# An attention and mixer kernel on one core: the first batch's v by casting transfers of GpSimd, later loads, shared PSUM tiles and whole-block squares

## The chip, the core and the metric

The kernel runs on one core of a Trainium2 chip. The core has five engines with a queue of instructions each: TensorE (PE, matmuls, with its weight loads shown as PEld), VectorE (DVE), ScalarE (ACT), GpSimd (Pool) and SyncE (SP), which here only issues transfers. Sixteen DMA engines move the data. SBUF is the memory on the core with 128 partitions; PSUM takes the matmuls' sums. The metric is device time in microseconds (us) of one execution.

## The reference

The batch is 8, the sequence S = 3136, the model width D = 256, the width of the queries and keys 64. All inputs and the result are float32; the kernel works in bfloat16 between them.

```python
scale = 1.0 / S
scores = scale * np.matmul(z, z.transpose(0, 2, 1))   # per batch: S x S
attn = np.maximum(scores, 0.0) ** 2
x = u * np.matmul(attn, v)                            # x: S x 256

h = (xT @ U @ V)T                                     # U: S x 32, V: 32 x S
u2 = x + h
result = u2 + np.maximum(u2 @ w_ch1, 0.0) @ w_ch2     # w_ch1: 256 x 1024
```

The keys and the queries are the same z, so the scores are symmetric: a block of keys against queries is the transpose of the mirrored block.

## The kernel before, in words

The 3136 rows of a batch are 24 tiles of P = 128 rows and a tail of 64. Queries go in groups of GW = 512 columns: NQ = 6 full groups and a seventh of 64 (NG = 7 groups to a batch). One pass of the main loop is a *slot* t, a batch and group (b, g); there are 56. In a slot PE computes attention times v for its group, scores for groups to come, and, a batch later, the mixer's part for group t − 7 and t − 8 (x + h, called u2, then w_ch1 and w_ch2).

**Blocks of scores.** A block holds four key tiles by 512 queries, 128x4x512 bf16, and stands in one of 20 SBUF buffers `blk`. It is made in two halves. For each half `score_pairs` runs two matmuls side by side, each on 64 of PE's rows (`pair`, the matmul at L184), into a PSUM tile `ps` of two banks (there are four such tiles). `rectify` then chooses ACT (L399) or DVE (L395) for relu and scale, PSUM to SBUF, and `score_finish` books the half's square on DVE for when the relu is done (`square`, L364, 128x1024). A half can be used by PE once it is squared. In the first slot `rectify` instead takes its ways from a list: "half" (ACT and DVE take one bank each of the same PSUM tile, relu at L376 and L377, square at L380 and L381) for the first two pairs, then "both", then "dve" (`one_pass`, L406: relu and square on DVE).

**The order.** The kernel is written with its own model of time. `clock` counts what PE has been given, `free_at` what the other engines have, `book` adds a piece of work to an engine, and `hold(time, f)` keeps a step back until the clock reaches that time; a step is put in its engine's queue when `run_held` comes to it. The order in which steps are issued is the order in each engine's queue. A queue is worked off in that order, so a transfer at SP that has to wait holds up those behind it. Blocks that are used from their mirrored side are turned by transposing DMAs (`issue_turn`, L421 and L429), and the tile z of later batches too.

**Mixer inputs.** x (L749, DVE, in bf16 as `x_bf`) plus h gives u2; its transpose `u2T` comes from a transposing DMA on SP (`x_turn`, L785), and PE multiplies it with w_ch1. `u2T` of the first group is needed first when slot 7 ends.

**Loads.** SP issues all transfers from device memory. `load_part` loads z and v of the next batch, `load_u` one group's u, `first_loads` the constants: U in slot 2, V in 3 and 4, w_ch1 in 5, w_ch2 in 6 (`load_w`). Up to slot 7 the loads are held to the slot's clock plus 5, and each next one 22 later; u to plus 60. Loads give float32; casts to bf16 are held in the next slot (`casts_next`).

**The first batch.** z comes in three pieces and v in six of four tiles, each staged as float32 in blocks: z (L1274, L226), v (L1274, L256) and the tails of 64 rows (L220) alternate on SP. z is cast on DVE and ACT (first piece), on Pool (second; L242) and on DVE (third). v's six pieces are cast by Pool (`cast_v`, L1261), the first straight away and the others as `spare` steps between other work. PE turns the cast z (`z_turn`, L331) and ACT copies the result into `zzT` (L340). Before that PE runs 21 empty matmuls (L1300). Then three score jobs are issued one by one (L1314 to L1316), and the main loop starts.

A GpSimd `nop` (L174) links two matmuls on different row halves of one PSUM bank; it is put in Pool's queue in the order of issue.

The following listing gives the functions that the change touches.

## Time and profile before

| | us |
|---|---|
| median of 3 runs | 982.09 (981.95 to 982.22) |
| profiled execution, device time | 986.39 |
| its span on the core | 984.6 |
| TensorE busy, share of the span | 973.7 (99%) |
| VectorE busy | 628.2 (64%) |
| ScalarE busy | 482.4 (49%) |
| GpSimd busy | 15.2 (2%) |

Mean granted TensorE clock: 0.998. The profile lists, for groups of instructions by line and operation, the output and input buffer, the sizes, the count, the busy time, and what ended the idle time before them. The chain that ended last follows the work back from the end through whatever released each step. The timeline lists instructions in order with start, duration, engine, line, operation, count, and in brackets how long the engine sat idle before and which piece of work ended it. An engine named with a q is its sequencer: SPq is the issue of transfers from SP's queue. Durations of transfers are given from issue to landing. Times of a timeline count from the start of the span.

### The profile page before, as it was taken

How to read it: one execution, taken by the hardware profiler on the slowest of the kernel's cores; microseconds unless marked ns; L12 is line 12 of the kernel's file. 1: busy time of each engine (PE TensorE's matmuls, PEld its weight loads, DVE VectorE, ACT ScalarE, POOL GpSimd, SP SyncE). 2: the span in 40 equal slices, each digit the busy share in tenths (PEclk: the TensorE clock that was granted, in tenths of full speed). 3: DMA queues.
4: the chain of work that ended last, by engine and by line, in shares of the span. 5: the costliest groups of instructions: out<-in, count | busy, mean ns of one | idle time of the engine just before them, and what ended most of it. 6: DMA issues, size and time to landing. Idle time of an engine off the chain costs nothing.

```text
span 984.6 us, 35373 instructions
## 1 busy us (share of the span) xinstructions
PE 973.7 (99%) x16163; PEld 773.4 (79%) x16163; DVE 628.2 (64%) x811; ACT 482.4 (49%) x565; POOL 15.2 (2%) x25
## 2 busy tenths in 40 slices
PE   8999899999999999999999999999999999999998
PEld 5788677877778778787777877788777887778766
DVE  6878755668556685566755667556775567653363
ACT  7877642456324473355633555334654346431353
POOL 4200000000000000000000000000000000000000
PEclk9999999999999999999999999999999999999999
DMA  8899999979997799987999879997799978965153
GB/s 269 193 225 192 228 196 188 223 153 197 195 204 167 160 192 192 205 170 170 185 208 207 154 178 179 223 189 153 173 207 206 194 144 163 186 135 95 55 114 99
DMA packets 372405, 176.37 MB, mean 179 GB/s; under 512 B 347296, under 2 KB 350624, under 8 KB 372256
## 3 DMA queue, kind: packets, MB, share of 16 engines
q1 hardware_dynamic: 372256, 174.12, 85.6%
q8 instruction: 126, 2.06, 0.9%
q14 instruction: 23, 0.19, 0.1%
HBM read 62.56 MB, written 25.69 MB: 90 GB/s over the span
## 4 chain that ended last, share of the span: by engine, by line
PE 96%; DVE 1%; ACT 1%; DMA 1%; issue 0%; DVEq 0%
PE ps L184 93%; PE ps L714 1%; DMA u2T<-x_bf 1%; PE ps L797 1%; ACT blk L399 0%; PE ps L1096 0%; DVE blk L364 0%; PE ps L1300 0%; PE ps L331 0%; DVE blk L377 0%; DVE blk L381 0%; DVE x_bf L749 0%; DVE blk L406 0%; DVE out_sb L870 0%; DVE blk L395 0%
## 5 line engine op out<-in xcount | busy, mean ns | idle before, releaser
L184 PEld LDWEIGHTS <-blk 64*128 64x128 bf16 x12288 | 609.7, 94 | 159.9 <-POOLq L174 9.6
L184 PE MATMUL ps<-v_bf,blk 64*128 64x256 bf16 x9216 | 613.0, 269 | 2.3 <-DVE blk L364 1.1
L399 ACT ACTIVATE blk<-ps 128x1024 bf16<-128x1024 f32 (+1 forms) x335 | 315.3, 970 | 346.6 <-PE ps L184 343.2
L364 DVE TENSOR_TENSOR blk<-blk 128x1024 bf16<-128x1024 bf16 x350 | 221.1, 656 | 49.1 <-ACT blk L399 48.4
L184 PE MATMUL ps<-u2T,w_bf 64*128 64x512 bf16 (+1 forms) x1792 | 227.9, 350 | 2.8 <-DMA u2T<-x_bf 2.8
L184 PE MATMUL ps<-w_bf,blk 64*128 64x256 bf16 x3072 | 192.0, 269 | 0.0
L959 DVE TENSOR_SCALAR blk<-ps 128x1024 bf16<-128x1024 f32 x105 | 128.5, 1224 | 97.6 <-PE ps L184 96.6
L962 ACT ACTIVATE blk<-ps 128x1024 bf16<-128x1024 f32 x87 | 88.3, 1022 | 119.0 <-PE ps L184 118.8
L184 PE MATMUL ps<-zzT 64*128 64x512 bf16 (+2 forms) x902 | 129.8, 327 | 0.6 <-ACT zzT L340 0.6
L184 PEld LDWEIGHTS <-w_bf 64*128 64x128 bf16 x1792 | 84.3, 94 | 30.2 <-POOLq L174 5.0
L749 DVE TENSOR_TENSOR x_bf<-ps,u_sb 128x1024 bf16<-128x1024 f32 x48 | 58.7, 1222 | 71.4 <-PE ps L184 71.4
L870 DVE TENSOR_TENSOR out_sb<-ps,x_bf 128x1024 f32<-128x1024 f32 x42 | 51.4, 1224 | 58.1 <-PE ps L184 58.1
L1082 DVE TENSOR_TENSOR out_sb<-ps,out_sb 128x1024 f32<-128x1024 f32 x42 | 51.4, 1224 | 18.6 <-PE ps L184 18.3
L184 PEld LDWEIGHTS <-zzT 64*128 64x128 bf16 x902 | 41.2, 94 | 6.9 <-ACT zzT L340 1.5
L184 PE MATMUL ps<-t_sb,V_bf 64*128 64x256 bf16 x200 | 20.6, 269 | 0.0
L395 DVE TENSOR_SCALAR blk<-ps 128x1024 bf16<-128x1024 f32 (+1 forms) x14 | 16.6, 1185 | 5.9 <-PE ps L184 5.1
L206 DVE CAST v_bf<-stage 128x1024 bf16<-128x1024 f32 (+1 forms) x30 | 18.5, 617 | 0.0
L184 PE MATMUL ps<-v_bf,last_sb 64*128 64x256 bf16 x192 | 18.5, 269 | 0.0
L204 ACT CAST v_bf<-stage 128x1024 bf16<-128x1024 f32 (+1 forms) x18 | 18.1, 1005 | 0.0
L206 DVE CAST x_bf<-out_sb 128x1024 bf16<-128x1024 f32 x22 | 15.2, 689 | 0.3
L1082 DVE TENSOR_TENSOR blk<-ps,blk 128x1024 f32<-128x1024 f32 x5 | 6.1, 1225 | 11.9 <-PE ps L184 11.8
L204 ACT CAST x_bf<-out_sb 128x1024 bf16<-128x1024 f32 x13 | 13.5, 1037 | 0.0
(83 smaller groups left out, 239.1 us busy)
## 6 DMA issues: line engine op xcount, KB each, us to landing
u_sb<-in_u_dram SPq DMA_DIRECT2D x48, 512.0 KB, 5.1
stage<-in_v_dram SPq DMA_DIRECT2D x42, 512.0 KB, 6.1
out_dram<-out_sb SPq DMA_DIRECT2D x42, 512.0 KB, 3.1
stage<-in_z_dram SPq DMA_DIRECT2D x7, 512.0 KB, 5.9
blk<-in_v_dram SPq DMA_DIRECT2D x5, 512.0 KB, 6.3
out_dram<-blk SPq DMA_DIRECT2D x5, 512.0 KB, 2.6
blk<-blk SPq DMA_TRANSPOSE x156, 5.1
blk<-in_moe_w_ch_dram SPq DMA_DIRECT2D x4, 512.0 KB, 4.9
```

The source lines that it names most:

```text
L184: ins = nc.tensor.matmul(**args)
L204: nc.scalar.copy(out=out, in_=in_)
L206: nc.vector.tensor_copy(out=out, in_=in_)
L364: nc.vector.tensor_tensor(out=a, in0=a, in1=a, op=ALU.mult)
L395: nc.vector.tensor_scalar(out=dst, in0=src, scalar1=scale, scalar2=0.0, op0=ALU.mult, op1=ALU.max)
L399: nc.scalar.activation(out=dst, in_=src, func=AF.Relu, scale=scale)
L714: nc.tensor.matmul(out=ps[c * hp : c * hp + rows, h, :D], lhsT=smalls[b][h * hp : (h + 1) * hp, place_of(jt), :], rhs=v_bfs[b][h * hp : (h ...
L749: nc.vector.tensor_tensor(out=xs[b, g][:rows, :n, :], in0=four(box["ps"])[:rows, :n, :], in1=u_sbs[b, g][:rows, :n, :], op=ALU.mult,)
L870: nc.vector.tensor_tensor(out=o[:rows, :n, :], in0=four(ps)[:rows, :n, :], in1=x, op=ALU.add)
L959: nc.vector.tensor_single_scalar(out=r, in_=ps[:, :, :gw], scalar=0.0, op=ALU.max)
L962: nc.scalar.activation(out=r, in_=ps[:, :, :gw], func=AF.Relu)
L1082: nc.vector.tensor_tensor(out=o, in0=acc, in1=o, op=ALU.add)
```

## The change

There are five parts.

1. The first batch's v is loaded by Pool's own queue, with the cast from float32 to bf16 done by the transfer: seven transfers (two of 128x512 for the first piece, five of 128x1024), straight into `v_bf`. The staging blocks and Pool's casts of v go. On SP the second and third z pieces, the tails and the first u follow one another.
2. The first two score jobs use `shared_pairs`: the pairs' banks are spread over two PSUM tiles, `a` and `d`, so that ACT takes its bank from `a` and DVE its bank from `d`. The way "half" of `rectify` goes.
3. For blocks of batch 0 of which the first half is finished in slots 1 to 5, the half's square is left out, and after the second half one square covers the whole block (`whole_block`, 128x2048).
4. w_ch2 is loaded in slot 7 instead of 6; a slot's `first_loads` stand ahead of the next batch's steps; in slot 7 the loads are held to the clock plus 78 and each next one 12 later; u is held to plus 5 in slot 6 and to plus 88 in slot 7; the casts in slot 8 to 45, and in slot 7 no longer to 60 but to 15.
5. One of the two casts of the third z piece goes from DVE to Pool.

```diff
-    ways = ["half", "half", "both", "dve"]
+    ways = ["both", "dve"]

+    halves, merged = {}, set()
+
+    def whole_block(n, key, turn):
+        waiting[0] -= 1
+        if n == 2:
+            square(blocks[key][1], 11.7)
+            squared[key] = 2
+        if turn:
+            hold(clock[0] + 7, lambda: ready_turns.append(turn))
+
     def score_finish(made):
...
+            if key and not key[0]:
+                n = halves[key] = halves.get(key, 0) + 1
+                if n == 1 and 0 < slot[0] < NQ:
+                    merged.add(key)
+                if key in merged:
+                    finish = lambda n=n, key=key, turn=turn: whole_block(n, key, turn)
             hold(whole or done, finish)

+    def shared_pairs(jobs):
+
+        (ka, a), (kb, d) = take_ps(), take_ps()
+        for i, (b, g, (J, h)) in enumerate(jobs):
...
+                nc.tensor.matmul(
+                    out=(a if jj == i else d)[:, jj, :],
...
+            dst = blocks[b, g, J][1][:, 2 * h : 2 * h + 2, :]
+            x, y = dst[:, i], dst[:, 1 - i]
+            nc.scalar.activation(out=x, in_=a[:, i], func=AF.Relu, scale=scale)
+            nc.vector.tensor_scalar(out=y, in0=d[:, 1 - i], scalar1=scale, scalar2=0.0, op0=ALU.mult, op1=ALU.max)
+            nc.scalar.activation(out=x, in_=x, func=AF.Square)
+            nc.vector.tensor_tensor(out=y, in0=y, in1=y, op=ALU.mult)
...
-        6: lambda: load_w(1),
+        NG: lambda: load_w(1),
...
     def first_v(i):
-        load_v_piece(0, i, vraw[i][1])
+        for t0 in range(i * GT, (i + 1) * GT, GT // 2 if i == 0 else GT):
+            n = GT // 2 if i == 0 else GT
+            nc.gpsimd.dma_start(out=v_bfs[0][:, t0 : t0 + n, :], in_=rows_of(v[0])[:, t0 : t0 + n, :])
+        v_cast.add((0, i))
...
-    for h in range(2):
-        load_run(vraw[0][1], v[0], D, h * GT // 2, GT // 2)
+    for i in range(NQ):
+        first_v(i)
     first_z(1)
-    first_v(1)
     first_z(2)
-    first_v(2)
-    first_v(3)
...
-    first_v(4)
-    first_v(5)
     load_u(*items[0])
-    cast_v(0, on_pool)
     cast_z(1, 0, on_pool)
     cast_z(1, 1, on_pool)
-    spare += [lambda i=i: cast_v(i, on_pool) for i in range(1, NQ)]
...
-    score_burst(jobs0[:1])
-    score_burst(jobs0[1:2])
+    shared_pairs(jobs0[:2])
     score_burst(jobs0[2:3])
...
-            hold(clock[0] + (90 if g_now == NQ and b_next > 1 else 60 if t == NG else 15 if t >= NQ else 45) + 12 * i, f)
+            hold(clock[0] + (90 if g_now == NQ and b_next > 1 else 45 if t == NG + 1 else 15 if t >= NQ else 45) + 12 * i, f)
...
-        steps += first_loads[t]() if t in first_loads else []
+        steps = (first_loads[t]() if t in first_loads else []) + steps
...
-                hold(clock[0] + 5 + 22 * i, lambda f=f: load(f))
+                hold(clock[0] + (78 + 12 * i if t == NG else 5 + 22 * i), lambda f=f: load(f))
         if t <= NG:
-            hold(clock[0] + 60, lambda t=t: load_u(*items[t + 1]))
+            hold(clock[0] + (5 if t == NQ else 88 if t == NG else 60), lambda t=t: load_u(*items[t + 1]))
...
-                qm.append((20, 0, False, lambda: (cast_z(2, 0, on_dve), cast_z(2, 1, on_dve), book("dve", 0, 8))))
+                qm.append((20, 0, False, lambda: (cast_z(2, 0, on_pool), cast_z(2, 1, on_dve), book("dve", 0, 4))))
```

More of the change, by code (lines that the diff above doesn't have):

```diff
@@ L374, in rectify @@
             way = ways.pop(0) if ways else min(ends, key=lambda w: ends[w])
-            if way == "half":
-                nc.scalar.activation(out=dst[:, 0], in_=src[:, 0], func=AF.Relu, scale=scale)
-                nc.vector.tensor_scalar(
-                    out=dst[:, 1], in0=src[:, 1], scalar1=scale, scalar2=0.0, op0=ALU.mult, op1=ALU.max
-                )
-                nc.scalar.activation(out=dst[:, 0], in_=dst[:, 0], func=AF.Square)
-                nc.vector.tensor_tensor(out=dst[:, 1], in0=dst[:, 1], in1=dst[:, 1], op=ALU.mult)
-                done = max(book("act", ready, 5.2), book("dve", ready, 6.2))
-                return done, max(book("act", ready, 5.2), book("dve", ready, 3.5))
             if way == "dve":
@@ L539, in score_burst, with finish @@
         score_finish(score_pairs(jobs))
+    def shared_pairs(jobs):
+        (ka, a), (kb, d) = take_ps(), take_ps()
+        for i, (b, g, (J, h)) in enumerate(jobs):
+            zzT = zzTs[b]
+            if h == 0:
+                blocks[b, g, J] = take_block()
+            for jj in range(2):
+                key = J * GT + 2 * h + jj
+                nc.tensor.matmul(
+                    out=(a if jj == i else d)[:, jj, :],
+                    lhsT=half(zzT, jj, key * P, P),
+                    rhs=half(zzT, jj, groups[g][0], GW),
+                    start=True,
+                    stop=True,
+                )
+            pe(GW / 256)
+            dst = blocks[b, g, J][1][:, 2 * h : 2 * h + 2, :]
[4 more added lines that the diff above has]
+            nc.vector.tensor_tensor(out=y, in0=y, in1=y, op=ALU.mult)
+            ps_free[ka] = book("act", clock[0] + 3, 5.2)
+            ps_free[kb] = book("dve", clock[0] + 3, 6.2)
+            book("act", 0, 5.2)
+            book("dve", 0, 3.5)
+            def finish(key=(b, g, J)):
+                squared[key] = squared.get(key, 0) + 1
+            hold(max(free_at["act"], free_at["dve"]), finish)
     def place_of(jt):
@@ L1243 @@
     zraw = [(i * 2 * GT, 2 * GT + (i == 2), *stage_block()) for i in range(3)]
-    vraw = [stage_block() for _ in range(NQ)]
     on_act, on_dve, on_pool = nc.scalar.copy, nc.vector.tensor_copy, nc.gpsimd.tensor_copy
     def first_v(i):
-        load_v_piece(0, i, vraw[i][1])
+        for t0 in range(i * GT, (i + 1) * GT, GT // 2 if i == 0 else GT):
+            n = GT // 2 if i == 0 else GT
+            nc.gpsimd.dma_start(out=v_bfs[0][:, t0 : t0 + n, :], in_=rows_of(v[0])[:, t0 : t0 + n, :])
+        v_cast.add((0, i))
     def first_z(i):
@@ L1256, in cast_z @@
         z_copy(0, t0 + lo, hi - lo, raw[:, lo * dqk :], c, copy)
-    def cast_v(i, copy):
-        raw = vraw[i][1].rearrange("p (t d) -> p t d", d=D)
-        for h in range(0, GT, GT // 2):
-            copy(out=v_bfs[0][:, i * GT + h : i * GT + h + GT // 2, :], in_=raw[:, h : h + GT // 2, :])
-        v_cast.add((0, i))
-        give_block(vraw[i][0])
     def cast_tail():
```

## The prediction

> **What bounds the kernel now.** I read the page's busy shares and its chain that ended last, then that chain in order of time, then windows and timelines where it leaves TensorE (PE).

> ```profile
> PE 973.7 (99%) x16163; PEld 773.4 (79%) x16163; DVE 628.2 (64%) x811; ACT 482.4 (49%) x565; POOL 15.2 (2%) x25
> ...
> PE 96%; DVE 1%; ACT 1%; DMA 1%; issue 0%; DVEq 0%
> ```

> PE is busy for 99% of the span and carries 96% of the chain. The change leaves PE's count of matmuls and, but for the first two pairs, nearly all of their order as they are, so it can only act where PE stands still. The matmuls show three such places over 0.8 us before 130 us: after 5.60 (1.10), after 26.34 (1.06) and after 108.43 (2.97), with some lesser ones up to 11.57. All else is cover. The chain (start, us, what) shows the first and the last; the line of dots stands for 91 us:

> ```profile
> 6.13 0.70 DVE blk L377
> 6.85 0.42 DVE blk L381
> 7.28 0.70 DVE blk L377
> 8.00 0.86 DVE blk L381
> 8.86 1.14 DVE blk L406
> 10.03 1.49 DVE blk L364 x2
> 11.57 2.64 PE ps L184 x40
> ...
> 102.97 8.44 DMA u2T<-x_bf
> 111.45 87.65 PE ps L184 x1396
> ```

> From 6.13 to 11.57 VectorE (DVE) runs without a pause and PE starts in earnest when it is done. At 102.97 it is a transfer: the first transpose of x into u2T, 8.44 us.

> **Part 1, the loads round the first x turn.** SyncE's (SP's) timeline, start and duration of each issue:

> ```profile
> 99.10 0.78 SPq L226 DMA_DIRECT2D stage<-in_z_dram  x1
> 99.93 0.42 SPq L1190 DMA_DIRECT2D blk<-in_moe_w_ch_dram  x1
> 100.39 0.50 SPq L226 DMA_DIRECT2D stage<-in_z_dram  x1
> 100.94 1.09 SPq L308 DMA_DIRECT2D u_sb<-in_u_dram  x2
> 102.97 2.25 SPq L785 DMA_TRANSPOSE u2T<-x_bf  x1
> ```

> Five loads (512 KB each, one of 256) go out in the 3 us ahead of the transpose; the last landed at 110.53, the transpose at 111.41. The tile's view gives issue to landing as 2.3 least, 3.6 median, 8.4 most (this one). The windows show the price; columns are us, then busy time of PE, its weight loads, DVE, ScalarE (ACT) and GpSimd (Pool), the granted clock, DMA share, GB/s:

> ```profile
> 108.40:114.50 6.10, 3.34 (x30) 1.74 (x28) 2.33 (x3) 0.42 (x1) 0.00 (x0) 0.72 1.02 176
> 114.50:122.00 7.50, 7.50 (x116) 5.39 (x114) 5.64 (x7) 6.86 (x10) 0.00 (x0) 1.00 0.75 207
> ```

> 30 matmuls took 6.10 us; at the next stretch's rate (116 in 7.50) they take 1.94. So 4.2 us hang on this transfer: 2.8 of stall, and 1.3 because the granted clock fell to 0.72 and pairs took 0.21 us apiece instead of 0.107.

> In the changed program SP's order round it is: one u load (formerly two), last_sb's transpose, one small block transpose, u2T's, and only then w_ch2's halves, u, z's two pieces, u, v. The casts of V and w_ch1 stay ahead. The small transpose's input is ready some 3 us earlier, so u2T's is issued as soon as x_bf is done (102.9) and, at the median of 3.6, lands at 106.5; PE asks at 108.43. **Gain 4.2**, with 1.9 us to spare. What is late next: w_ch2 (asked for at 127.4, issued some 22 us ahead, its loads land in 4.9 in the median), the next batch's z and u, behind it on the same queue; their first users are over 10 us away. Nothing waits.

> **Part 2, whole-block squares.** 19 blocks of batch 0 lose two squares of 128x1024 and get one of 128x2048 after the second half. That saves DVE a fixed cost each (656 ns per 1024 columns in the groups, 0.99 for one of 1600, so I estimate 1.21 for 2048 instead of 1.31), under PE: nothing. What it costs is time ahead: half a block is no longer ready while the other is being scored. I took, for each of the 19, the gap from its second score pair to its first use by PE. All but one have 3.65 to 19 us and need about 3 (relu 1, square 1.2, latencies). The exception is the first:

> ```profile
> 27.57 0.38 PE L184 MATMUL ps<-zzT 64*128 64x512 bf16 x2
> ...
> 28.00 4.77 ACT L399 ACTIVATE blk<-ps 128x1024 bf16<-128x1024 f32 x5 [0.98 <-PE ps L184]
> ...
> 29.05 1.25 DVE L364 TENSOR_TENSOR blk<-blk 128x1024 bf16<-128x1024 bf16 x1 [1.05 <-ACT blk L399]
> ```

> Its second pair runs at 27.57, and PE uses the first half at 28.12. After the change that use waits for ACT's relu (28.00 to 28.98) and the square of 2048 (29.03 to 30.24): PE goes on at 30.25, **a loss of 2.13**. The next such block is used 0.2 to 0.45 late as well, against two stalls there (0.22 and 0.21) that the new one absorbs. **Net cost 2.1**, 1.7 to 2.5. Queued behind the square on DVE is only a relu; behind PE's wait stand score pairs whose ACT and DVE work is thereby early, not late. Low bound: 0, if PE's order or the squares' lets another block go first; nothing I see allows it. Can the clock fall too? The stall of 1.06 left pairs at full rate, that of 2.97 did not; 2.1 lies between, nearer to 1.06: I take nothing and keep +1.4.

> [...]

> **Part 3, the start.** In the chain above, DVE's first relu waits until 6.13 for ACT's read of the same PSUM tile (2.29 idle). Two tiles let it begin when pair 0 is done, at 5.47. Then by the same durations: relu 6.16, square 6.58, second relu (pair 1 waits for the tiles' first readers, about 6.6) 7.31, square 7.75 (0.42; the 0.86 stood beside a Pool cast), one pass to 9.1, two squares to 10.5: PE's 11.57 becomes 10.55, **−1.0**.

> But Pool's queue is now in the way. SP loses seven v issues (3.1 us of 0.43 to 0.5 each), so z's second piece is issued at 1.6 instead of 2.6. Pool gets the seven, casting, and behind them its two casts of that z (1.17 together), which a PE turn, an ACT copy (1.0) and PE's pairs wait for: 2.4 us from cast end 8.59 to pair 10.97. Before, Pool's sum was one v cast and then a wait for z. The page has no casting DMA and no Pool DMA, so the issue cost g is unknown. Bounds: 0.43 (SP's issue) to 1.17 (Pool's pair of casts). With issues from 1.35 the casts end at 2.5+7g: 5.5 at 0.43, 10.7 at 1.17, against 8.59 now. The turn limits the start when 7g exceeds 6.0. At 1.17 the start is 1.2 late after the gain is gone. I take about 0.6 (Pool's single cast is the nearest row), which leaves the DVE chain as the limit.

> [...]

> Next, v itself: PE needs its six pieces at 6.81, 11.57, 13.83, 16.74, 19.77 and 22.45; they landed at 5.2, 9.1, 11.3, 13.0, 14.9 and 16.2, 512 KB per 1.64 us (320 GB/s). Afterwards 3.15 MB on Pool's queue run beside 2.0 to 2.8 MB that SP issues without waiting. At an even half, 160 GB/s, pieces land at about 9.6, 12.9, 16.2, 19 and 20.7: just in time for a start 0.8 earlier. **So I take −0.8.** The price of v's cast on Pool (8.3 us in six pairs) goes; it hid beside PE. DVE gives z's last cast (0.4) to Pool, which is idle then.

> **Part 4, nothing.** Later batches keep their order; the tail from 920 us on is the same.

> **Sum**: −4.2 + 2.1 − 0.8 = −2.9. The profiled execution took 986.39 (span 984.6), 4.3 above the median of 982.09; the sum is 983.5 against it, and by the same difference **979.2** against the median. 0.2%, about 2.0 us, is what a measurement here can tell from no change.

> **Rivals.**
> - Squares cost nothing, since the 27.57 block is covered after all: 982.1 − 4.2 − 1.0 = 976.9. For: other blocks have 3.65 and more. Against: the order of instructions. 0.10.
> - The stall of 2.1 also halves the clock, +1.4: 980.6. For: 0.72 after 2.97. Against: full rate after 1.06. 0.08.
> - u2T's transpose still waits for the queue: the 4.2 stays, 983.4. For: six other SP issues stand near it. Against: none of the five loads is ahead of it. 0.04.
> - Pool's issues or v's transfers run behind by a little: the start changes by +0.2 to +3.9, 980.2 to 983.9, say 981.0. For: the single margins worked out above. 0.17.
> - Slower: Pool's seven issues cost 1.6 us or more apiece. z's second piece is then cast at 13.7 and the start is 4.2 late, which with −4.2 and +2.1 passes 2.0; at 2.0 apiece it is 7.0 late, 987.0. DVE's casts and squares beside Pool are the means: a DVE square took 0.86 beside a Pool cast, 0.42 without, and a Pool pair 2.04 instead of 1.17. The same sign if v comes at under 120 GB/s (the last piece after 26.6). Against: both bounds of g lie below 1.6. 0.17.

> [...]

> **How the numbers follow.** The forecast has 0.44, its own range 978.2 to 980.4 (1.0 less to 1.2 more by the squares' and the start's bounds). Leaving out the slower rival (0.17) above and a little below gives 976.9 to 983.4. Faster by over 0.2% (under 980.1): most of 0.44, the 0.10 and a little of the late start, 0.53. Slower: 0.17. Within: 0.30.

> **What would show it.** Right: u2T's first transpose lands in under 5 us and no PE idle near 108; a PE stall of about 2 us at 27 with the releaser DVE L364, its form 128x2048; DVE's first relu near 5.5; PE's long run from about 10.6. Wrong: v's landing, or Pool's z casts, as what ends PE's waits before 25 us; a granted clock under 1.0 after the stall at 27.

## The result, and the profile after

The change made the kernel slower by 0.4%: 986.49 us in the median of 4 runs (985.99 to 988.01) against 982.02 (981.93 to 982.22), ratio 1.0043 with a 95% interval of 1.0031 to 1.0056. Forecast were 979.2 and a range of 976.9 to 983.4; the time lies outside it, on the side that had 0.17. The profiled execution took 988.01, its span is 986.2.

The page after, busy shares and the chain by engine:

```profile
PE 975.1 (99%) x16163; PEld 775.9 (79%) x16163; DVE 626.6 (64%) x794; ACT 481.7 (49%) x562; POOL 10.3 (1%) x21
...
PE 96%; DVE 1%; ACT 1%; DMA 1%; issue 0%; SPq 0%; DVEq 0%
```

PE is the bound as before. Since its matmuls come in nearly the same order, the start of the n-th matmul after, less that of the n-th before, shows where time goes. Between the two profiled executions that offset is +0.6 at 19 us, +0.4 at 26, +4.0 at 33, −0.4 at 115 (all of u2T's stall gone), +1.3 at 130, +1.6 from 191 on. So the two *profiled* executions differ by 1.6, while the *median* times differ by 4.5. That gap is the main thing to explain, beside the four places. A wait is given here, as in the prediction, as the time from one matmul's start to the next, less the 0.05 us that a matmul takes up (0.11 at half rate). The brackets of the timeline count from the modelled end of the matmul before and give 0.2 to 0.5 less.

**The start.** The chain in order of time, after (start, us, what):

```profile
5.60 0.70 DVE blk L569
6.31 0.04 issue
6.35 0.61 PE ps L558 x2
6.96 3.41 PE ps L184 x28
10.37 0.58 PE ps L331 x8
10.95 0.02 issue
10.97 1.02 ACT zzT L340
```

The stretch from 6.8 to 10.3 (us, then busy time of PE, PEld, DVE, ACT, Pool, the granted clock, DMA share, GB/s), the change first and then, from a run further down, its start alone:

```profile
6.80:10.30 3.50, 3.50 (x30) 2.13 (x26) 2.73 (x5) 2.17 (x4) 0.00 (x0) 1.00 1.15 223
6.80:10.30 3.50, 2.94 (x45) 2.01 (x44) 3.43 (x6) 3.00 (x4) 0.61 (x1) 1.00 1.14 224
```

DVE's first relu starts at 5.60 instead of 6.13, as meant. But pair 1 waits until 6.35 for DVE's read of the shared tile (1.31, or 0.81 idle by the timeline), and then 28 matmuls take 3.41 us: a pair took 0.21 instead of 0.107. Half rate is how PE begins in every kernel here: its first empty matmuls and turns of z take 0.107 apiece, later ones 0.055, and the change from one to the other came between 3.8 and 6.0 us in every profile but that of the change. There it came at 10.37. PE itself is now the chain up to the turn, where before it was DVE.

**The first whole block.** The chain after, from its second half's relu on, PE's timeline at its end, and the windows, the last line that of the kernel before:

```profile
28.38 1.03 ACT blk L390
29.43 1.24 DVE blk L364
30.72 48.22 PE ps L184 x786
```

```profile
30.72 0.31 PE L184 MATMUL ps<-v_bf,blk 64*128 64x256 bf16 x2 [2.05 <-DVE blk L364]
```

```profile
28.40:30.70 2.30, 0.26 (x6) 0.00 (x0) 1.23 (x1) 1.00 (x1) 0.00 (x0) 1.00 0.85 274
30.70:34.30 3.60, 3.58 (x30) 2.17 (x32) 0.46 (x1) 1.94 (x2) 2.03 (x2) 0.53 0.15 58
30.70:34.30 3.60, 3.60 (x56) 2.36 (x54) 3.60 (x6) 3.13 (x5) 1.02 (x2) 1.00 0.09 34
```

PE waits 2.27, near the 2.13 worked out, and then goes on at a granted clock of 0.53: 30 matmuls in 3.60, which before took 56 in the same stretch.

**The first x turn.** SP's timeline after:

```profile
104.01 1.19 SPq L412 DMA_TRANSPOSE blk<-blk  x1
106.97 1.93 SPq L825 DMA_TRANSPOSE u2T<-x_bf  x1
108.95 0.58 SPq L1230 DMA_DIRECT2D blk<-in_moe_w_ch_dram  x1
```

The transpose goes ahead of the loads, and PE's wait for it, 2.97 before, is gone; PE's whole list of waits has one for a u2T, of 0.2, at 190.98. (It is part of the last step in the offset above, from +1.3 to +1.6.)

**A new wait at 127.** SP's, DVE's, ACT's and PE's timelines after:

```profile
114.41 7.33 SPq L420 DMA_TRANSPOSE blk<-blk  x1
121.83 1.21 SPq L412 DMA_TRANSPOSE blk<-blk  x1
123.10 1.97 SPq L220 DMA_DIRECT2D stage<-in_z_dram  x2
125.11 1.24 SPq L220 DMA_DIRECT2D stage<-in_v_dram  x2
```

```profile
121.54 1.22 DVE L999 TENSOR_SCALAR blk<-ps 128x1024 bf16<-128x1024 f32 x1
122.67 0.68 DVE L206 CAST x_bf<-out_sb 128x1024 bf16<-128x1024 f32 x1
126.65 0.75 DVE L206 CAST z_bf<-stage 128x576 bf16<-128x576 f32 x1 [3.29 <-DMA stage<-in_z_dram]
127.32 1.28 DVE L364 TENSOR_TENSOR blk<-blk 128x1024 bf16<-128x1024 bf16 x2
128.52 0.29 DVE L206 CAST v_bf<-stage 128x256 bf16<-128x256 f32 x1
128.72 1.22 DVE L999 TENSOR_SCALAR blk<-ps 128x1024 bf16<-128x1024 f32 x1
```

```profile
126.53 0.67 ACT L204 CAST z_bf<-stage 128x576 bf16<-128x576 f32 x1 [2.31 <-DMA stage<-in_z_dram]
127.10 1.93 ACT L390 ACTIVATE blk<-ps 128x1024 bf16<-128x1024 f32 x2
```

```profile
128.17 1.49 PE L184 MATMUL ps<-w_bf,blk 64*128 64x256 bf16 x24 [1.02 <-ACT blk L390]
130.00 0.61 PE L184 MATMUL ps<-w_bf,blk 64*128 64x256 bf16 x8 [0.34 <-DVE blk L999]
```

The moved z loads drag their 64-row tails with them, which are held another 75 of the kernel's own clock and then queue behind a block's transpose. Two casts that read the tail are already in the queues: DVE stands 3.29 us in front of one, ACT 2.31 in front of the other. The relus behind them that PE needs come late: ACT's (L390) ends a stall of 1.23, the mixer's on DVE (L999) one of 0.55.

### The profile page after: what moved, and what is told of

It is laid out like the page before. It is cut to its first block, busy times and chain, and to the rows that moved or that the text cites. A ratio compares the mean times of both kernels' runs of the same rounds, so it can differ in the third digit from the quotient of the medians.

```text
span 986.2 us, 35349 instructions
## 1 busy us (share of the span) xinstructions
PE 975.1 (99%) x16163; PEld 775.9 (79%) x16163; DVE 626.6 (64%) x794; ACT 481.7 (49%) x562; POOL 10.3 (1%) x21
## 4 chain that ended last, share of the span: by engine, by line
PE 96%; DVE 1%; ACT 1%; DMA 1%; issue 0%; SPq 0%; DVEq 0%
PE ps L184 93%; PE ps L754 1%; PE ps L837 1%; ACT blk L390 0%; PE ps L1136 0%; DMA u2T<-x_bf 0%; DVE blk L364 0%; PE ps L1328 0%; PE ps L331 0%; DVE blk L999 0%; DMA stage<-in_z_dram 0%; SPq L420 0%; SPq L220 0%; DVE out_sb L910 0%; DVE x_bf L789 0%
## 5 line engine op out<-in xcount | busy, mean ns | idle before, releaser
L184 PEld LDWEIGHTS <-blk 64*128 64x128 bf16 x12288 | 612.1, 94 | 161.1 <-POOLq L174 10.3
L184 PE MATMUL ps<-v_bf,blk 64*128 64x256 bf16 x9216 | 614.2, 270 | 2.9 <-DVE blk L364 2.9
L390 ACT ACTIVATE blk<-ps 128x1024 bf16<-128x1024 f32 (+1 forms) x333 | 313.1, 967 | 345.4 <-PE ps L184 343.0
L364 DVE TENSOR_TENSOR blk<-blk 128x1024 bf16<-128x1024 bf16 (+2 forms) x331 | 218.4, 682 | 48.1 <-ACT blk L390 47.1
L184 PE MATMUL ps<-u2T,w_bf 64*128 64x512 bf16 (+1 forms) x1792 | 227.6, 350 | 0.2 <-DMA u2T<-x_bf 0.2
L184 PE MATMUL ps<-w_bf,blk 64*128 64x256 bf16 x3072 | 192.3, 269 | 1.4 <-ACT blk L390 1.0
L999 DVE TENSOR_SCALAR blk<-ps 128x1024 bf16<-128x1024 f32 x105 | 128.5, 1224 | 93.2 <-PE ps L184 92.3
L184 PE MATMUL ps<-zzT 64*128 64x512 bf16 (+2 forms) x898 | 130.2, 329 | 0.6 <-ACT zzT L340 0.6
L184 PEld LDWEIGHTS <-w_bf 64*128 64x128 bf16 x1792 | 84.5, 94 | 27.4 <-POOLq L174 5.0
L184 PEld LDWEIGHTS <-zzT 64*128 64x128 bf16 x898 | 41.1, 95 | 6.0 <-ACT zzT L340 0.8
L386 DVE TENSOR_SCALAR blk<-ps 128x1024 bf16<-128x1024 f32 x16 | 19.6, 1224 | 9.7 <-PE ps L184 9.6
L184 PE MATMUL ps<-t_sb,V_bf 64*128 64x256 bf16 x200 | 20.6, 269 | 0.0
L184 PE MATMUL ps<-v_bf,last_sb 64*128 64x256 bf16 x192 | 18.5, 269 | 0.0
L204 ACT CAST v_bf<-stage 128x1024 bf16<-128x1024 f32 x15 | 15.6, 1040 | 0.0
L206 DVE CAST x_bf<-out_sb 128x1024 bf16<-128x1024 f32 x22 | 15.2, 690 | 0.3
```

The costliest lines, as they stand in the source:

```text
L184: ins = nc.tensor.matmul(**args)
L204: nc.scalar.copy(out=out, in_=in_)
L206: nc.vector.tensor_copy(out=out, in_=in_)
L364: nc.vector.tensor_tensor(out=a, in0=a, in1=a, op=ALU.mult)
L386: nc.vector.tensor_scalar(out=dst, in0=src, scalar1=scale, scalar2=0.0, op0=ALU.mult, op1=ALU.max)
L390: nc.scalar.activation(out=dst, in_=src, func=AF.Relu, scale=scale)
```

## The experiments

All timed comparisons below are with runs of the kernel before on the same chip (982.7 to 982.8 in the median there, single executions from 981.6 to 986.7).

**Before, once more.** No edit.

> The kernel before, unchanged, profiled a second time. Theory A: the stall ahead of the first u2T (2.97 us, with half rate behind it worth 4.2) belongs to its profiled execution of 986.39, and the timed ones at 982.0 do not have it: then a second profiled execution either shows it again with a time near 986.4, or is free of it with a span near 980.4 and a time near 982. Theory B: the stall is in every execution, and the 4.3 us between 986.39 and 982.09 are spread over the span: then the stall stands there in this profile too, while its time is near 982.

Its profiled execution took 984.37, span 982.6. The chain, PE's timeline and the window behind:

```profile
103.03 7.84 DMA u2T<-x_bf
```

```profile
110.91 0.61 PE L184 MATMUL ps<-u2T,w_bf 64*128 64x512 bf16 x4 [2.16 <-DMA u2T<-x_bf]
```

```profile
111.00:115.00 4.00, 4.00 (x60) 2.81 (x60) 1.45 (x3) 2.62 (x4) 0.00 (x0) 1.00 1.16 174
```

Neither theory as put: the stall is there again, but 2.37 instead of 2.97, and no half rate follows (60 matmuls in 4.00, clock 1.00). The two profiled executions differ by 2.0 in time and by 2.0 in PE's offset behind 114 us. So this stall varies from one execution to the next, and the first profile of before had a large one.

**The moved loads alone.**

```diff
-        6: lambda: load_w(1),
+        NG: lambda: load_w(1),
...
+        steps = (first_loads[t]() if t in first_loads else []) + steps
...
+                hold(clock[0] + (78 + 12 * i if t == NG else 5 + 22 * i), lambda f=f: load(f))
...
+            hold(clock[0] + (5 if t == NQ else 88 if t == NG else 60), lambda t=t: load_u(*items[t + 1]))
```

(and the line on the casts, as in the change)

> Only part 4, the moved loads. Theory A (timed executions of before never had the u2T stall): no gain, 982.0 to 983.8, the loss being the two PE stalls at 127 and 129 (1.23 and 0.55 in the profile after) that the late z tails bring through DVE's queue. Theory B (they had it): -4.4 + 1.8 = -2.6, 979.4.

983.52 against 982.75, ratio 1.0010 (1.0001 to 1.0019): 0.8 slower. Its profile has no u2T stall and the two stalls behind the tails' casts, 1.12 and 0.55. That is in theory A's range; a gain of 2.6 is excluded. Its premise, that timed executions of before have no such stall at all, does not hold up in the next run.

**The moved loads, tails at once.**

```diff
-            if b > 1:
+            if b > 2:
                 hold(clock[0] + 75, tails)
```

> The moved loads, but the tails of batch 2's z and v issued right behind z and not 75 of the clock later. Theory: the two stalls at 127 and 129 in the profile after (1.6 us with what they bring) are DVE standing before the tails' cast; they are gone from the profile, and the time is 1.6 under that of the moved loads alone, 0.8 under before (982.0 if before is at 982.8). Rival: the stalls come from the loads of w_ch2 or u instead; then they stay, and the time is that of the moved loads, 0.8 over before.

982.03 against 982.83, ratio 0.9985 (0.9974 to 0.9996): 0.8 faster, and 1.5 faster than with late tails. SP's, DVE's and ACT's timelines of this kernel:

```profile
107.30 1.11 SPq L220 DMA_DIRECT2D stage<-in_z_dram  x2
```

```profile
118.99 0.74 DVE L206 CAST z_bf<-stage 128x576 bf16<-128x576 f32 x1
```

```profile
119.81 0.68 ACT L204 CAST z_bf<-stage 128x576 bf16<-128x576 f32 x1
```

The tails go out 12 us earlier than in the moved loads alone (119.17), neither cast waits, and the stalls are gone. What is left, 0.8, I take as the median worth of the u2T stall, since nothing else differs by design from before; its executions lie within 0.6 of each other (981.63 to 982.21), where those of before spread over 4.

**More ahead of the x turn.** To ask from the other side, one load more in front of the transpose:

```diff
             raw = stage()
+            if b == 2 and t0 == 0:
+                entry, more = stage_block()
+                nc.sync.dma_start(
+                    out=more.rearrange("p (t d) -> p t d", d=dqk), in_=rows_of(z[b])[:, t0 : t0 + n, :]
+                )
+                give_block(entry)
```

> The kernel before with one more load of 512 KB (z of the next batch, into a block that is not read) ahead of the first u2T transpose on SP's queue. Theory: the transpose waits for what stands ahead of it, and in timed executions of before it is just about late (0.8 us over all): 512 KB more at the 320 GB/s of the start cost 1.6, and up to 3.3 where the half clock follows; 984.4 to 986. Rival: in timed executions the transpose has room, its lateness belongs to profiled ones: under 0.5.

984.06 against 982.70, ratio 1.0011 (1.0000 to 1.0023); single executions from 981.88 to 987.33, those from 985.5 up with a mean clock of 0.998. The medians differ by 1.4, a little under the 1.6 expected, and the interval touches no change: it leans to the theory without proving it. The execution of 985.90 that was profiled has a stall of 2.60 with a clock of 0.60 behind:

```profile
111.00:115.00 4.00, 4.00 (x36) 2.31 (x38) 0.18 (x1) 1.22 (x2) 0.00 (x0) 0.60 1.00 190
```

**Whole-block squares alone.** `whole_block`, `halves` and `merged` as in the change.

> Only part 3, whole-block squares. In the profile after PE's offset against before grows by 3.6 between 26 and 33 us: 2.3 of stall at the first merged block, 1.7 of half clock behind it, less the two small stalls that it takes in. Theory A and B alike: +3.6, 985.6. My prediction's own step: +2.1, 984.1.

986.93 against 982.75, ratio 1.0037 (1.0024 to 1.0049), by medians +4.2. Its profiled execution took 985.38, the others 985.33 to 988.14. In the profiled one the wait is again 2.27, but the window behind it reads

```profile
30.40:34.00 3.60, 3.60 (x58) 2.73 (x60) 1.91 (x2) 2.87 (x4) 2.03 (x2) 1.00 0.10 38
```

58 matmuls at full clock. Its mean clock is 1.000, while the three executions from 986.9 up have 0.998 or 0.996. Where the clock fell in these three can't be seen, but in the change's profile it fell behind this very wait. So the same wait lowers the clock in some executions and not in others.

The traces say more on when. Each holds a record of the moments at which the clock changes, and in every one of the 14 these lie whole multiples of 3.413 us apart: 5.32, 111.13 and 114.54 in before (31 and 1 of them), 10.37, 30.85 and 34.27 in the change (6 and 1). Cut at these steps, once the clock has first risen, PE's idle time within one step, every wait counted, was 2.00, 2.20, 2.43 and 2.45 us ahead of the four falls in the midst of a run (casts alone, more ahead, before, the change) and 1.75 at most (before once more) where none followed. The change's wait at 28 lies whole in one step; that of the squares alone, just as long, falls across two and leaves 1.44 and 1.46 in them. No run moved a wait across a step on purpose, so this is read from the traces and not tested.

**The first block excepted.**

```diff
-                if n == 1 and 0 < slot[0] < NQ:
+                if n == 1 and 0 < slot[0] < NQ and key != (0, 1, 2):
```

> Whole-block squares for all the blocks but the first of slot 1, which keeps its two squares. Theory: that one block carries the whole loss of 4.2, so the time is that of before within 0.5, and PE's stall at 28 is gone. Rival: the other 18 blocks cost as well (less time ahead, longer squares in front of other DVE work): over 1.0 above before.

983.62 against 982.83, ratio 1.0007 (0.9998 to 1.0016). The stall at 28 is gone; the next whole block of that slot still waits 0.75 where before it waited 0.22. The 0.8 lies between the 0.5 of the theory and the 1.0 of the rival, and the interval does not exclude no loss. So by medians the first block carries most of the loss, 3.4 of 4.2, and of the other 18 one more is seen to be late.

**PE busy over that wait.** All the whole-block squares, and

```diff
+            if (b, g, jt // GT) == (0, 1, 2) and not filled:
+                filled.append(1)
+                now = clock[0]
+                k, f = take_ps()
+                for _ in range(28):
+                    nc.tensor.matmul(out=f[:, 0, :P], lhsT=blank, rhs=blank, start=True, stop=True)
+                clock[0] = ps_free[k] = now
             pair(
```

> Whole-block squares, and 28 empty matmuls of 128x128 in PE's queue ahead of the first use of slot 1's first block, so that PE is busy while it waits. Theory: the loss of 4.2 is 2.2 of waiting and, in most executions, some 1.7 of half clock behind it; the wait stays, the half clock goes: 2.2 over before in every execution, spread under 1.5. Rival: the clock is not what the idling does; the time stays at 4.2 over before, with single executions from 2.6 to 5.4.

984.23 against 982.83, ratio 1.0012 (1.0003 to 1.0021), all executions between 983.90 and 984.48. The timeline of this kernel:

```profile
28.12 1.74 PE L703 MATMUL ps<-blank 128*128 128x128 bf16 x28
28.96 1.23 DVE L364 TENSOR_TENSOR blk<-blk 128x2048 bf16<-128x2048 bf16 x1 [1.65 <-ACT blk L399]
30.24 0.28 PE L184 MATMUL ps<-v_bf,blk 64*128 64x256 bf16 x2 [0.38 <-DVE blk L364]
```

The useful matmul starts as late as without the filling (30.24), yet the loss falls from 4.2 to 1.4 and the spread from 2.8 to 0.6. So here it was the idling that lowered the rate: no execution has a mean clock under 0.999, where three of five had 0.998 or 0.996 without the filling. That 1.4 remain and not 2.2 fits the x turn: PE comes 2.2 later to the transpose, and this profile has no u2T stall over 0.4.

**The start alone.** Casting transfers, shared pairs and the cast moved to Pool, loads and squares as before.

> Parts 1, 2 and 5, the start: v by Pool's casting transfers and the pairs over two PSUM tiles. In the profile after PE's offset is +0.4 by 26 us, with PE at half rate from 6.7 to 10.3. Theory S (the pairs' wait at 4.93 to 6.35 lowers the clock): +0.4, 982.4, with the same half rate. Rival (the half rate came from elsewhere in the change): full rate, -0.8, 981.2.

982.65 against 982.75, ratio 1.0003 (0.9990 to 1.0016), but single executions from 980.79 to 986.09: eight up to 983.4 with mean clocks from 0.999, three from 985.4 with 0.997 or 0.998. The chain of the profiled one (981.59):

```profile
6.21 0.39 PE ps L542 x2
6.60 1.96 PE ps L184 x28
```

The same 28 matmuls as above in 1.96 instead of 3.41. At full rate the start is worth what the steps said: PE's offset against before is −1.1 at 19 us. At half rate the change had +0.6 there. So of the two profiled executions one began at half rate and one did not; the record of the clock has its first rise at 5.45 here, ahead of most of the pairs' wait, and at 10.37 in the change, where the steps of 3.413 us ended at 6.96 and 10.37. Before has a wait of the same 0.82 idle half a microsecond later, and no profile shows it with such a step.

The three executions from 985.4 up are not explained by this. Half rate at the start costs 1.7 (from −1.1 to +0.6) and not 4 to 5, and it leaves no mark in the mean clock: the change's 0.998 is accounted for by its one fall at 30.85, though it also began at half rate. A mean of 0.997 or 0.998 needs a fall later in the run. This kernel still has its loads ahead of u2T's transpose, and so the likelier cause, not shown by a profile of such an execution, is the stall there.

**The start, PE busy between the pairs.**

```diff
+            if i == 0:
+                kc, c = take_ps()
+                for _ in range(10):
+                    nc.tensor.matmul(out=c[:, 0, :P], lhsT=blank, rhs=blank, start=True, stop=True)
+                ps_free[kc] = clock[0]
```

> The start's parts alone, with ten empty matmuls of 128x128 between the two shared pairs, where PE waits 0.8 for the first readers of the two tiles. Theory: half clock after that wait makes some executions 4 to 5 us slower than others (980.8 to 986.1 without the filling); with it all are near the fast ones, 1.1 to 1.5 under before, spread under 2. Rival: the slow ones come from the transfers of v and z and stay: the spread is 5, the median level with before.

981.85 against 982.83, ratio 0.9992 (0.9984 to 1.0001): 1.0 under by medians, ten of eleven executions between 981.19 and 982.49, one at 984.72 with a clock of 0.997. In the profile of the repaired kernel further down, with the same filling, the empty matmuls go from 0.107 to 0.056 apiece at 5.8, so the rate rises in the midst of them; in this kernel's own profile it had risen before them, at 4.64. Against the kernel without the filling the spread shrinks from 5.3 to 3.5, where the theory had under 2. With u2T's stall still in both kernels, and one execution over 984 here against three there, it is not shown that the filling did it.

**The casting transfers alone.** With part 5: `first_v` on Pool's queue, no `cast_v`; the pairs as before.

> Part 1 alone (with part 5): v by Pool's casting transfers, the first two pairs as before. Theory: the DVE chain keeps its wait for ACT until 6.13, and only the square beside Pool's cast (0.86) gets shorter (0.42): 0.4 under before, spread under 2.5 since the shared pairs' wait is not there. Rival: v or z's second piece come late by Pool's queue: 0.5 or more over before.

982.14 against 982.70, ratio 0.9999 (0.9988 to 1.0010). By medians 0.6 under, by the interval undecided; v and z's second piece are not late in its profile. The spread is 3.4, where 2.5 was expected. The execution profiled was one of the longest, 984.80, and it shows a u2T stall of 2.21 with the clock down behind it:

```profile
110.00:114.00 4.00, 4.00 (x40) 2.48 (x38) 0.00 (x0) 1.56 (x3) 0.00 (x0) 0.57 1.04 206
```

The shared pairs alone were not run.

**Both repairs together.** The start with its filling and the moved loads with the tails at once, squares as before.

> The start with the empty matmuls, and the moved loads with batch 2's tails at once; squares as before. Theory: the gains add, 1.0 and 0.8, and the earlier start makes the u2T stall that goes a little larger: 1.8 to 2.3 under before. Rival: the u2T transfer is where both gains come from, so they don't add: 1.0 under.

980.85 against 982.70, ratio 0.9978 (0.9969 to 0.9987), all within 980.52 to 981.62. It has the lowest median of the study: 1.9 under before. The gains add (1.0 and 0.8), which the rival denied. Of the four kernels with the moved loads and without the first whole block (the moved loads with late tails and at once, this one and the next) no execution lies more than 1.1 over its median or has a mean clock under 0.999. That fits the long executions being those with a long stall at u2T.

**And with whole-block squares from slot 2 on.**

```diff
-                if n == 1 and 0 < slot[0] < NQ:
+                if n == 1 and 1 < slot[0] < NQ:
```

> The same with whole-block squares for blocks whose first half is finished in slots 2 to 5. Theory: those have at least 5.8 us from second score pair to first use in this order, so the squares change nothing: level with the kernel of the same call without them, within 0.4. Rival: DVE's saved time brings something, or the longer squares hold up what is behind them: a difference over 0.5.

981.11 against 982.70, ratio 0.9981 (0.9972 to 0.9990): level with the kernel before it. This is the whole change with three repairs, and by medians of different sets of runs it is 5.4 under the change; each against its own runs of before, 1.0043 became 0.9981. Where a block has time ahead, one square instead of two makes no difference that can be told here (0.3 by medians).

## Why the prediction was wrong

The parts, each by itself against before, are about −0.1 (start), +4.2 (squares) and +0.8 (loads): 4.9, against 4.5 measured for all. By my steps:

**u2T's stall, −4.2: the mechanism right, its size in the median execution wrong.** The transpose did go ahead of the loads and the stall did vanish; between the two profiled executions it gave the full 4.4. But the sum failed where it was carried over: I took the 4.3 us between the profiled execution (986.39) and the median (982.09) as a constant that applies alike to before and after. They were mostly the very 4.2 us that I then took away. In the median execution the stall is worth 0.8. What made the execution profiled slow was the largest piece outside PE in its chain, so the page showed an unusual cost as if it were the usual one. Why the transpose comes later in some executions isn't settled: its landing took 8.44, 7.84, 6.70 and 6.04 in the profiles of before, before again, squares and start, with the loads issued at slightly different times ahead of it. In all four it lands 0.8 to 0.9 after the last of these loads (110.53, 110.00, 111.04 and 106.93), so it is the loads that come late. Both profiles of before lie above its median, but profiling doesn't always bring a long stall: four kernels that keep the loads ahead (squares, squares with the first block excepted, the start with and without filling) show 0.4 to 1.0 of idle there. What unprofiled executions did can't be seen, only that, of 88 of before beside these kernels, five have a mean clock under 0.999, like the profiled one of 986.39, and these are the five from 985.8 up.

**"Nothing waits" behind the moved loads: wrong, +1.6.** I named w_ch2, z and u as what would be late next and checked their first users on PE. I missed the tails, which `load_z_piece` holds back by a further 75, and the rule I had used elsewhere: who stands behind the waiting instruction on its engine. The casts on DVE and ACT are no one's bottleneck, but relus that PE needs stand behind them.

**Squares, +2.1: the place and the wait right (2.27 measured), the half clock wrong.** I had the rival with +1.4 and gave it 0.08, on the ground that 1.06 did not lower the clock and 2.97 did. With the change it came true, at 1.7 (offset +2.6 at the end of the wait, +4.3 at the end of the half rate). The length of the wait alone does not decide it: the same wait left the clock up in the profile of the squares alone. The second merged block took 0.75 in place of 0.22, a little more than the 0.2 to 0.45 foreseen.

**The start, −0.8: right at full clock (−1.1 at 19 us), lost in the change's profile to the rate, and level in the median.** Pool's seven issues took 3.85, 0.55 apiece where I chose 0.6, and its z casts ended at 6.58 where I had 6.7. The v transfers were in time. What failed is "pair 1 waits for the tiles' first readers, about 6.6": I counted that wait (it ended at 6.35) only in DVE's chain, and not as 1.3 us in which PE stands before its rate has risen. There was a slip in the chain too: by its own rows the one pass ends at 8.9 and not 9.1, so that PE would have started at 10.45 and not 10.55. That changes nothing in the outcome. Why the start alone is level in the median, when its profiled execution was 1.1 ahead at 19 us, stays open; part of the gain may be waited off again at u2T, which PE then reaches earlier.

**The slower rival** was put at Pool's queue, which needed 1.6 apiece. Its means, DVE's work beside Pool, did not bring that: DVE's three z casts ran from 2.90 in the midst of the seven issues, these took 0.55 apiece all the same, and it was the casts that took longer (1.13 against 0.79 before). So the 0.17 came true in its sign and not in its reason, which is luck. The sign came from elsewhere: with u2T's term at 0.8 and the half clock in, my own terms would have read −0.8 + 1.6 + 2.1 + 1.7 − 0.8 = +3.8.

## What to carry to other kernels

Before a stall of the profile is subtracted from the median, hold the profiled execution against the timed ones: if it lies above them by about what the stall costs, the stall may be what sets that execution apart. A wait of PE has two prices, its length and the rate behind it; where a step adds one of about 2 us or more, put the second price in as a likely case (it came behind 2.21, 2.27, 2.60 and 2.97 here, at 1.3 to 1.7, and not behind another 2.27 and 2.37), or fill the gap with empty matmuls. A wait in the first microseconds, before the rate has risen, may put that rise off (it came at 10.37 us in the change, at 5.32 before); look for it too. And when a load is moved, follow every transfer of its step, the small ones too, to the cast that reads it and then to what is queued behind that cast.
